# Q and K projected densely and read back into head slots, gated tiles paired in a bank, VectorE units in the first two chunks dropped

## The chip, the cores and the metric

The kernel runs on one core of a Trainium2 chip. The metric is the device time of one execution in microseconds. Four compute engines matter: TensorE (PE in the profile; PEld is its weight load), ScalarE (ACT), VectorE (DVE) and GpSimd (POOL). SyncE (SP) issues all the DMAs of this kernel.

## The reference

A transformer layer over S = 2048 rows of D = 640, H = 32 heads of Dh = 20, F = 1728, all in bf16:

```python
h  = x + attention(layernorm(x), wqkv) @ wo     # softmax(q k^T * 20**-0.5) v, not causal
z  = layernorm(h)
h2 = h + ((z @ w_gate) * (z @ w_up)) @ w_down
```

The layernorms have no weights. The scores are 32 x 2048 x 2048 values; their exponentials are the largest single piece of work.

## The kernel before, in words

**Slots.** A head has only 20 rows, so Q and K are kept transposed with each head in a slot of 32 partitions (`SLOT`), four heads to a group of 128 partitions, eight groups (`NG`). Row 20 of a slot holds a constant, 1 for K and `BETA` = 394 for Q, so that each score gets the same offset; rows 21 to 31 are zero. `qa[g]` holds the first three blocks of 512 queries, `qb[g]` the fourth, `kT[g]` all keys. V lies with the keys on the partitions in `vx`, 21 columns a head, the last of them a one, so that P·V also gives the softmax sums.

**Iterations.** The middle of the kernel is a sequence of iterations, one exponential on ScalarE each (L658). A unit is 128 keys by 512 queries of one head. Its scores are one matmul over the slot's 32 rows (L650); the units of different heads that are issued together use different row quarters of TensorE. Iterations take three units (128x1536, tile `sc0`) and two units (128x1024, `sc1`) in turn; the results are the `E` tiles, four and three of them. Some units don't go to ScalarE: `on_dve` (L366) says how many of a segment are computed by VectorE. Their score goes into a bank of a two-bank ring `mi`, from which L670 converts it to 16-bit integers (`di`); two such units make a batch of three more VectorE steps (L553 `dm`, L555 `dt`, L558 the product), and the exponential is the sum of the products of `dt` and `di` with V. `due` spreads these units over the iterations of their segment.

**Segments.** A segment is a head group with a range of keys and of queries. Query block 0 runs first: for groups 0 to 3 (`G1` = 4) key chunk by key chunk (four chunks of 512 keys), then groups 4 to 7 over all keys. Blocks 1 to 3 follow, each with some groups over 512 queries and the rest in two halves of 256.

**P·V and its end.** The products (L788) of one segment go into the only `acc` bank, 32 columns a head. `close` (L803) copies it into `asb` (L812), a single buffer for 512 queries. `norm` (L681) then runs on SP and POOL: the sums are written to DRAM (L688) and read back spread over partitions (L689), eight iterations later POOL takes the reciprocal (L692), it is written (L694) and read back broadcast with four DMAs (L697), and nine iterations after that POOL scales `asb` into `On` (L701), which frees `asb`.

**The queue of jobs.** Between the scores of iterations TensorE gets other work from one ordered queue (`add`, `do`, `peek`): transposes of the layernormed rows, projections, output projection (`job_out`), the gated layer (`job_glu`, L1098) and the down projection (`job_y`, L1111). A planner at build time keeps modelled clocks for TensorE and VectorE and issues a job's next piece when it fits; where the queue is empty it fills with matmuls on `ident` whose result isn't used. `ensure(key)` forces a job to its end when an iteration or a product needs its result. All matmuls of these jobs go through `by_cols` (L267), which splits 128 output rows into four pieces of 32, each on its own column quarter; a job uses one `mi` bank, evacuated by VectorE.

**Projections.** `job_proj` (L321) makes Q or K of one group and one chunk of 512 rows: five 128-row steps times four column pieces, 20 matmuls, from weights `wpad` in which each head's 20 columns are spread to slots of 32. `evac_b` adds the constant row (L245) and writes the slot layout. The padded weights are made from `wqk` by copies on ScalarE and POOL (`pad_half`) for all eight groups; `wqk` lies in tiles borrowed from `E` and `wo`. The padding tiles are zeroed by memsets on VectorE (L180). `job_V` (L333) makes one half of V for 128 rows. Order in the queue: per chunk the transposes, then V half 0 and Q, K of groups 0 to 3 in turn; then groups 4 to 7 of block 0 and of K, with V half 1; then Q of blocks 1 to 3, with the loads of `wo` (four DMAs a group, L962) behind the Q jobs of block 1; then one `spill` step per group, which copies Q to DRAM (`qsp`), where a slower fallback path can read it. Before block 3, `load_res` puts gated weights of four column groups into the tiles of `qa`.

**Gated layer and tail.** For two 128-row tiles at a time (256 columns), `glu_sum` (L1079) computes one 128-column block of `up` or `gate` in one bank: 27 weight blocks of 128 columns or 64, of which the up ones are copied to `u` (L238) and the gate ones multiplied with it (L1093). The last two tiles of block 3 are done after all exponentials; there (`last_tail`, from L1173) matmuls are 128 wide instead of 4 x 32.

## Time and profile before

| | |
|---|---|
| median of 3 executions | 891.98 us (890.58 to 893.82) |
| the profiled execution | 893.23 us |
| its span | 891.3 us |
| mean granted TensorE clock | 0.992 |
| instructions | 34572 |
| busy: PE, VectorE, ScalarE, POOL | 836.2, 717.6, 805.9, 196.2 us |
| DMA | 52.04 MB, mean 58 GB/s |

How to read the rows. In the groups a row is: line, engine, operation, output tile and input tile, shapes and types, count; then total busy time and the mean of one in ns; then the idle time of the engine right before these instructions and what ended most of it. In the timeline a row is: start, length (us), engine, line, operation, tiles, shape, and how many instructions were merged in the row; what it waited for stands in brackets. The table of windows has, for each stretch, its length, the busy time and count of PE, PEld, VectorE, ScalarE and POOL (or, where one line is asked for, of that line's engine alone), then the mean granted clock, the DMA share and GB/s. The digits of the slices are busy tenths in 40 equal parts of the span. The row for a DMA line gives issue times; the one of an engine's waits gives who waited for whom and for how long.

### The profile page before, as it was taken

To read this page: it belongs to the slowest core of one execution; us is meant where nothing else is said; L and a number is where in the kernel's file an instruction comes from. 1 tells how busy PE (TensorE), PEld (TensorE's weight loads), DVE (VectorE), ACT (ScalarE), POOL (GpSimd) and SP (SyncE) were. 2 spreads that over 40 slices of the span, in tenths; PEclk is the share of its full clock that TensorE was granted. 3 is DMA by queue.
4 is the path that set the end of the run, shared out by engine and by line. 5 is a ranking of instruction groups with operands and counts; after the bars stand their busy time and mean duration, and the time that the engine had idled before them with its cause. 6 is when DMAs were issued, how large, how long until landed. Compare 5 with 4: busy or idle time off the path is not lost.

```text
span 891.3 us, 34572 instructions
## 1 busy us (share of the span) xinstructions
PE 836.2 (94%) x15346; PEld 410.1 (46%) x15346; DVE 717.6 (81%) x1470; ACT 805.9 (90%) x719; POOL 196.2 (22%) x263
## 2 busy tenths in 40 slices
PE   6899999998989899999999999999999999999997
PEld 4334343332324334445445555555444555555775
DVE  7684578998879988987989889888987899888642
ACT  5899999998999999999999999999998999999431
POOL 3210034221123321221312233112310242113000
PEclk8999999998999999999999999999999999999999
DMA  6000001010053152101323132303600320031310
GB/s 200 9 25 1 3 16 40 20 36 12 14 203 104 42 146 74 37 17 31 95 70 95 29 92 71 96 22 98 154 4 22 88 55 16 10 104 39 82 46 19
DMA packets 85883, 52.04 MB, mean 58 GB/s; under 512 B 23664, under 2 KB 82592, under 8 KB 85728
## 3 DMA queue, kind: packets, MB, share of 16 engines
q1 hardware_dynamic: 85728, 49.77, 20.6%
q8 instruction: 122, 2.00, 1.0%
q14 instruction: 33, 0.27, 0.1%
HBM read 42.43 MB, written 7.31 MB: 56 GB/s over the span
## 4 chain that ended last, share of the span: by engine, by line
PE 54%; DVE 24%; ACT 18%; issue 3%; DMA 1%; SPq 0%; POOL 0%; ACTq 0%; DVEq 0%; POOLq 0%
PE mi L267 23%; ACT E L658 18%; PE sc L650 13%; PE acc L788 11%; DVE di L670 7%; DVE di L558 3%; PE f L267 3%; DVE dm L553 2%; DVE st L199 2%; DVE dt L555 2%; PE mi L650 1%; DVE hh L1093 1%; DVE qa L245 1%; DVE kT L245 1%; PE acc L1260 1%
## 5 line engine op out<-in xcount | busy, mean ns | idle before, releaser
L658 ACT ACTIVATE E<-sc 128x1536 bf16<-128x1536 f32 (+2 forms) x683 | 788.4, 1253 | 29.1 <-PE sc L650 13.4
L670 DVE TENSOR_SCALAR di<-mi 128x512 int16<-128x512 f32 x342 | 232.9, 684 | 47.5 <-PE mi L650 42.8
L788 PE MATMUL acc<-E,vx 128*32 128x256 bf16 (+1 forms) x2540 | 222.6, 315 | 5.7 <-DVE asb L812 2.3
L650 PE MATMUL sc<-qa,kT 32*128 32x256 bf16 (+1 forms) x1808 | 206.4, 320 | 11.3 <-ACT E L658 8.1
L650 PEld LDWEIGHTS <-kT 32*128 32x128 bf16 x3072 | 84.6, 91 | 219.9 <-issue 211.9
L692 POOL TENSOR_TENSOR rr<-rr,powers 128x8 f32<-128x8 f32 (+1 forms) x44 | 97.4, 2214 | 284.1 <-DMA rr<-sums 284.1
L788 PEld LDWEIGHTS <-vx 128*32 128x32 bf16 x3604 | 84.1, 95 | 104.3 <-issue 94.1
L558 DVE TENSOR_TENSOR di<-di,dm 128x1024 bf16<-128x1024 bf16 x171 | 120.4, 704 | 3.6
L650 PE MATMUL mi<-qa,kT 32*128 32x256 bf16 (+1 forms) x368 | 96.0, 312 | 4.3 <-DVE qa L245 2.2
L267 PE MATMUL mi<-lnT,wp 128*32 128x512 bf16 x1240 | 90.7, 385 | 2.3 <-DVE di L670 0.9
L553 DVE TENSOR_SCALAR dm<-di 128x1024 int16<-128x1024 int16 x171 | 77.5, 453 | 2.9
L788 PE MATMUL acc<-di,vx 128*32 128x256 bf16 (+1 forms) x532 | 77.4, 307 | 0.1
L788 PE MATMUL acc<-dt,vx 128*32 128x256 bf16 (+1 forms) x532 | 76.0, 309 | 0.3 <-DVE dt L555 0.3
L555 DVE TENSOR_SCALAR dt<-di 128x1024 int16<-128x1024 int16 x171 | 72.9, 426 | 0.0
L650 PE MATMUL sc<-qb,kT 32*128 32x256 bf16 (+1 forms) x732 | 66.8, 288 | 4.2 <-ACT E L658 3.5
L267 PE MATMUL mi<-wd,hh 128*32 128x320 bf16 x1391 | 65.6, 300 | 1.0 <-DVE xr L1123 0.9
L267 PE MATMUL mi<-ln2T,wu 128*32 128x256 bf16 (+1 forms) x1170 | 54.6, 298 | 5.3 <-DVE ln2T L238 2.2
L267 PE MATMUL mi<-ln2T,wg 128*32 128x256 bf16 (+1 forms) x1170 | 54.8, 298 | 0.5 <-DVE u L238 0.3
L267 PEld LDWEIGHTS <-hh 128*32 128x32 bf16 (+1 forms) x1489 | 46.1, 96 | 18.7 <-issue 9.5
L1093 DVE TENSOR_TENSOR hh<-mi,u 128x256 bf16<-128x256 f32 (+1 forms) x84 | 38.9, 463 | 11.3 <-PE mi L267 10.4
L267 PEld LDWEIGHTS <-wp 128*32 128x32 bf16 x1240 | 31.0, 96 | 35.2 <-issue 19.4
L238 DVE CAST u<-mi 128x256 bf16<-128x256 f32 (+1 forms) x84 | 38.9, 464 | 9.6 <-PE mi L267 8.2
(130 smaller groups left out, 759.9 us busy)
## 6 DMA issues: line engine op xcount, KB each, us to landing
wu<-in_B_w_up_dram SPq DMA_DIRECT2D x29, 320.0 KB
wg<-in_B_w_gate_dram SPq DMA_DIRECT2D x29, 320.0 KB
bc<-scr SPq DMA_DIRECT2D x64, 64.0 KB
bc<-scr SPq DMA_DIRECT2D x112, 32.0 KB
qsp<-qa SPq DMA_DIRECT2D x8, 384.0 KB
xr<-in_A_x_dram SPq DMA_DIRECT2D x16, 160.0 KB
out_dram<-xr SPq DMA_DIRECT2D x14, 160.0 KB
wd<-in_B_w_down_dram SPq DMA_DIRECT2D x13, 160.0 KB
```

The source lines that it names most:

```text
L199: nc.vector.bn_stats(st[:, h, :], halves[h] if halves else src[:, h * HALF:(h + 1) * HALF])
L238: nc.vector.tensor_copy(dst, src)
L267: nc.tensor.matmul(out[k:k + w, :], lhsT=lhsT[:, k:k + w], rhs=rhs, **flags)
L553: nc.vector.tensor_scalar(m16[:, 0:n], s16, M_MASK, M_BITS, ALU.bitwise_and, ALU.bitwise_or)
L555: nc.vector.tensor_scalar(t16[:, 0:n], s16, E_MASK, E_BITS, ALU.bitwise_and, ALU.bitwise_or)
L558: nc.vector.tensor_tensor(sb[:, 0:n], sb[:, 0:n], mb[:, 0:n], ALU.mult)
L650: nc.tensor.matmul(dst[:, h * w:(h + 1) * w], lhsT=kT[g][SLOT * j:SLOT * (j + 1), (kt + h) * P:(kt + h + 1) * P], rhs=q_of(g, b, c0, w)[SL ...
L658: nc.scalar.activation(e[:, 0:n], sc[:, 0:n], ACT.Exp, bias=EXP_BIAS, scale=SM_SCALE)
L670: nc.vector.tensor_scalar(t[:, k * BANK:(k + 1) * BANK], sd[:], EXP_A, 0.0, ALU.mult, ALU.max)
L692: nc.gpsimd.tensor_tensor(ri, r16, powers[:, 1:2].to_broadcast([P, n]), ALU.pow)
L788: nc.tensor.matmul(acc["t"][SLOT * j:SLOT * (j + 1), 0:w], lhsT=vx[kt][:, VS * h:VS * h + SLOT], rhs=e, start=(j not in acc["new"]), stop= ...
L1093: nc.vector.tensor_tensor(st["hh"][2 * fp + f2][0:M, c0:c0 + n], ps[0:M, 0:n], hold["u"][0:M, 0:n], ALU.mult)
```

## The change

It has three parts that share tiles.

**Dense projections.** Q and K of most groups are no longer computed slot by slot. `job_dense(m, t, ch)` computes 128 dense columns (6.4 heads) of Q (m = 0) or K (m = 1) for one chunk, 20 matmuls straight from `wqk`; five such tiles replace eight jobs. VectorE copies the bank to `dn` (four buffers), and a DMA writes it to a DRAM tensor `dense[m]`. Once all tiles of a set of groups are written, `read_slots` reads them back with four DMAs, one for each head of a group, 20 rows x groups x 512, into the slots. `kT`, `qa` and `qb` become one tile each over all groups. The constant rows are filled at the start: two memsets of 128x1024 on VectorE, and eight DMAs. Groups 0 to 3 of chunk 0, and K of group 0 in chunk 1, stay with `job_proj`, so only four groups of weights are padded (`GP`), in five copies instead of ten. Scores contract over 21 rows of a slot (`VS`) instead of 32, since rows 21 to 31 are no longer written. `ensure_qk` forces the dense tiles and the read-back of a set that is needed. The queue has K tiles, then V half 0 for each chunk; then the other dense tiles of block 0 and of K; then all of V half 1; then dense Q of blocks 1 to 3 with the last three `wo` loads in block 1; then five `wo` loads and one `spill` step of eight DMAs of 21-row slices.

**Gated layer.** With 256 columns, two weight blocks of the same kind share a bank side by side (`glu_bank`, `job_glu`): one copy of 128x512 for `up`, one product of 128x512 for `gate`. The last column group has 128 + 64 columns; its 64-column blocks of up and gate share one bank, above each other. `hh` gets one tile per column group.

**VectorE units.** `D_CHUNK` was 2 for each group in chunk 3 alone; it is now 0 in chunks 0 and 1 and 2 in chunks 2 and 3.

```diff
-CHUNK_D = (3, 0)
-D_CHUNK, D_WHOLE, D_HALF, D_LAST = 2, 12, 6, 4
+GP = 4
+D_CHUNK = (0, 0, 2, 2)
+D_WHOLE = (12, 12, 12, 12)
+D_HALF = (0, 6, 6, 6)
...
+    dense = [dram.tile([D, S], BF16, name=f"dense{m}", bufs=1) for m in range(2)]
-    wqk = [e_tile(c) for c in range(KT)]
-    wpad = [ra.tile([P, 2, H, SLOT], BF16, name=f"wp{c}") for c in range(KT)]
+    wqk = [ra.tile([P, D], BF16, name=f"wqk{c}") for c in range(KT)]
+    wpad = [ra.tile([P, 2, GP * HPG, SLOT], BF16, name=f"wp{c}") for c in range(KT)]
...
+    for m, v in ((1, 1.0), (0, BETA)):
+        src = dp.tile([P, DW], I16, name="di", bufs=3)[:].bitcast(BF16)
+        nc.vector.memset(src, v)
...
+                nc.sync.dma_start(dst[DH:P:SLOT, g0:g1, x:x + w], src[DH:P:SLOT, None, 0:w].to_broadcast([HPG, g1 - g0, w]))
...
+    def job_dense(m, t, ch):
+        yield ROUND * KT
+        ps = bank()
+        for c in range(KT):
+            for k in range(0, P, SLOT):
+                col = t * P + k
+                nc.tensor.matmul(ps[k:k + SLOT, :], lhsT=wqk_half(c, col // HALF)[:, m, col % HALF:col % HALF + SLOT],
+                                 rhs=lnT[:, c, ch * QB:(ch + 1) * QB], start=(c == 0), stop=(c == KT - 1))
+            mm(ROUND)
...
+        dn = dnp.tile([P, QB], BF16, name="dn")
+        nc.vector.tensor_copy(dn[:], ps[:])
+        nc.sync.dma_start(dense[m][t * P:(t + 1) * P, ch * QB:(ch + 1) * QB], dn[:])
+        written[m, t, ch] = clk["dve"] + WRITE
+        for it in slot_sets:
+            if it["m"] == m and it["ch"] == ch and all((m, x, ch) in written for x in it["ts"]) and not it["on"]:
+                later(3, lambda it=it: read_slots(it))
...
+    def read_slots(it):
...
+        src = dense[m][:, ch * QB:(ch + 1) * QB].rearrange("(g j e) n -> j e g n", j=HPG, e=DH)
+        for j in range(HPG):
+            nc.sync.dma_start(dst[SLOT * j:SLOT * j + DH, g0:g1, c0:c0 + QB], src[j, :, g0:g1, :])
+        for key in it["keys"]:
+            done.add(key)
+            ready[key] = max([clk["pe"]] + [written[m, t, ch] for t in it["ts"]]) + READ
+
+    def ensure_qk(key):
+        if key not in done and key in slot_of:
+            it = slot_of[key]
+            for t in it["ts"]:
+                ensure(("dn", it["m"], t, it["ch"]))
+            read_slots(it)
+        ensure(key)
+        clk["pe"] = max(clk["pe"], ready.get(key, 0))
...
-            return D_CHUNK * int((lo // TPB, g) >= CHUNK_D)
+            return D_CHUNK[lo // TPB]
...
-                    lhsT=kT[g][SLOT * j:SLOT * (j + 1), (kt + h) * P:(kt + h + 1) * P],
-                    rhs=q_of(g, b, c0, w)[SLOT * j:SLOT * (j + 1), :],
+                    lhsT=kT[g][SLOT * j:SLOT * j + VS, (kt + h) * P:(kt + h + 1) * P],
+                    rhs=q_of(g, b, c0, w)[SLOT * j:SLOT * j + VS, :],
...
+    for m in (1, 0):
+        slots(m, G1, NG, 0)
+    for ch in range(1, NB):
+        slots(1, int(ch == 1), G1, ch)
+        slots(1, G1, NG, ch)
+        slots(0, 0, NG, ch)
...
+            if ch == 1:
+                add(need_T(("k", 0, ch), ch), job_proj(1, 0, ch))
+            for t in range(3):
+                dense_job(1, t, ch)
+            for t in ts:
+                value(t, 0)
...
+    for t in range(2, KT):
+        dense_job(0, t, 0)
+    for ch in range(NB):
+        for t in range(2 + (ch > 0), KT):
+            dense_job(1, t, ch)
+    for t in range(NT):
+        value(t, 1)
...
+        for t in range(KT):
+            dense_job(0, t, b)
+            if b == 1 and t + KT < NG:
+                do(("wo", t + KT), lambda g=t + KT: load_wo(g))
...
+        for j in range(HPG):
+            rows = slice(SLOT * j, SLOT * j + VS)
+            nc.sync.dma_start(qsp[j, :, :, 0:QA], qa_all[rows, :, :])
+            nc.sync.dma_start(qsp[j, :, :, QA:S], qb_all[rows, :, :])
...
-    def glu_sum(st, fp, f2, k, c0, n, hold):
+    def glu_bank(st, parts, c0, n, use):
...
+        for k, (col, tiles) in enumerate(parts):
+            w = SLOT if end["pool"] is None else P // len(tiles)
+            for c in range(KT):
+                r0 = 0
+                for wt, f0, m in tiles:
+                    for x in range(0, m, min(w, m)):
+                        d = min(w, m)
+                        nc.tensor.matmul(ps[r0 + x:r0 + x + d, col:col + n], lhsT=wt[:, c, f0 + x:f0 + x + d],
+                                         rhs=st["ln2T"][:, c, c0:c0 + n], start=(c == 0), stop=(c == KT - 1))
+                    r0 += m
...
+            elif fp == FP - 1:
+                yield from glu_bank(st, [(0, [(wu, 0, P)]), (n, mixed)], c0, n, up(fp, 0, n))
+                yield from glu_bank(st, [(0, [(wg, 0, P)])], c0, n, gate(fp, 0, 1))
+            else:
+                for w, use in ((wu, up(fp, 0, None)), (wg, gate(fp, 0, 2))):
+                    yield from glu_bank(st, [(f2 * n, [(w, f2 * P, P)]) for f2 in range(2)], c0, n, use)
```

More of the change, by code (lines that the diff above doesn't have):

```diff
@@ L1082, in glu_sum @@
         yield ROUND * KT * n // QB
         ps = bank()
[L1084 to L1096 removed]
+        last = len(parts) * KT
@@ L1098, in job_glu, with up, use @@
+        use(ps)
     def job_glu(st, ts, order=tuple(range(FP))):
         c0, n = ts[0] * P, len(ts) * P
-        hold = {}
+        per = QB // n
+        u_of = {}
+        def up(fp, f2, odd):
+            def use(ps):
+                u = u_of[fp] = late["s"].tile([P, QB], BF16, name="u")
+                w = n * min(per, 2)
+                evac("dve" if end["pool"] is None else "act", u[:, 0:w], ps[:, 0:w])
+                ev(w, held["slot"])
+                if odd is not None:
+                    half(fp, u, odd, ps)
+            return use
```

165 lines of the change are left out of this document (91 added, 74 removed).

## The prediction

> **What bounds the kernel now.** I read the page first (span, slices, chain), then the groups by form, ScalarE's idle time by stretches, and the timeline of both ends.
>
> ```profile
> span 891.3 us, 34572 instructions
> ACT  5899999998999999999999999999998999999431
> PE 54%; DVE 24%; ACT 18%; issue 3%; DMA 1%; SPq 0%; POOL 0%; ACTq 0%; DVEq 0%; POOLq 0%
> L658 ACT ACTIVATE E<-sc 128x1536 bf16<-128x1536 f32 x341 | 500.4, 1467 | 11.7 <-PE sc L650 7.4 <-PE mi L650 2.7
> L658 ACT ACTIVATE E<-sc 128x1024 bf16<-128x1024 f32 x341 | 355.0, 1041 | 17.3 <-PE mi L650 8.2 <-PE sc L650 6.0
> L658 ACT ACTIVATE E<-sc 128x512 bf16<-128x512 f32 x1 | 0.6, 597 | 0.0
> 17.95 3.71 ACT L658 ACTIVATE E<-sc 128x1536 bf16<-128x1536 f32 x3 [1.45 <-PE sc L650]
> 833.41 0.60 ACT L658 ACTIVATE E<-sc 128x512 bf16<-128x512 f32 x1
> ```
>
> The exponentials run from 17.95 to 834.0 us and ScalarE idles before them for only 11.7 + 17.3 = 29.0 us. So there are three parts: a head of 18 us, a stage that ScalarE bounds (816 us; TensorE only sets the 29), and a tail of 891.3 - 834.0 = 57.3 us in which ScalarE hardly matters. That PE has 54% of the chain says only that the chain passes through it between two exponentials. One iteration (one exponential with its scores) is (1467 + 1041) / 2 = 1.254 us.
>
> **The change part by part.** The profiled execution took 893.23 us, 1.25 above the median of 891.98; the sum is a difference and is applied to both.
>
> *DVE units.* 8 more of the 128x512 units go to VectorE, so ScalarE runs 340 + 339 exponentials instead of 341 + 341 + 1: 1467 + 2 x 1041 + 597 = 4.15 us less. This stage is ScalarE's: **-4.2**.
>
> *Projections.* The matmuls of Q and K fall from 1240 to 140 + 720 = 860.
>
> ```profile
> 203.71 1.26 PE L267 MATMUL mi<-lnT,wp 128*32 128x512 bf16 x20
> L245 DVE TENSOR_SCALAR kT<-mi,kb 128x512 bf16<-128x512 f32 x31 | 23.0, 743 | 19.1 <-PE mi L267 19.1
> 834.73 10.27 PE L267 MATMUL mi<-ln2T,qa 128*32 128x256 bf16 x300
> L670 DVE TENSOR_SCALAR di<-mi 128x512 int16<-128x512 f32 x342 | 232.9, 684 | 47.5 <-PE mi L650 42.8
> ```
>
> A job of 20 takes 1.26 us, so 380 fewer are 24 us of TensorE. 62 evacuations of 0.743 become 7 of them and 36 plain copies (0.684, by the di row, the same shape out of the same bank): 46.1 to 29.8 us. Against that VectorE gets 8 x 0.684 us of new units and four more three-step batches. All of it lies beside exponentials and is worth nothing by itself; it lets the queue of jobs be empty earlier, which counts in the tail.
>
> *Gated layer.* Pairing leaves the matmul count as it was, but the two 64-column pieces now fill one bank: 5 rounds less for each pair of tiles (20 matmuls take 10.27 / 15 = 0.68 us, so up to 0.7 us each), and two evacuations of half a bank become one of a whole (0.68). Beside ScalarE this can only thin out the late scores. Ends: -6 (a third of the 17 us of ScalarE idle time after 225 us) and +3 (gated jobs now stand where the queue was empty). I take **-2**, near nothing, since most of these gaps end on a score matmul behind a VectorE unit, and those stay.
>
> *A disturbed stretch.*
>
> ```profile
> 200.00:225.00 25.00, 20.81 (x19) 0.86 0.04 12
> 225.00:250.00 25.00, 24.49 (x22) 1.00 0.16 53
> 204.50 1.64 DVE L558 TENSOR_TENSOR di<-di,dm 128x1024 bf16<-128x1024 bf16 x1
> 206.85 0.37 PE L650 MATMUL mi<-qa,kT 32*128 32x512 bf16 x1 [1.57 <-DVE qa L245]
> 210.00:212.00 2.00, 2.00 (x19) 0.42 (x23) 1.95 (x4) 1.36 (x2) 0.00 (x0) 0.50 0.00 0
> ```
>
> The first two rows are the exponentials alone: 24.49 - 20.81 = 3.7 us were lost where a slow VectorE step held the evacuation of a projection, TensorE idled 1.57 us, and its granted clock then was 0.50. After the change no projection runs past iteration 139 (this was about 150). It may recur with another evacuation: ends -3.7 and 0, taken **-2**.
>
> The Trainium skill ("TensorE: Matmul & The Clock Gate", HAM oscillation) puts the gap that drops the clock above about 3.4 us; here 1.57 us was enough, and the trace decides. By the page a late read-back of 2 us would cost 2 us, by this row 2 + 3.7.
>
> *The read-back.* K of groups 1 to 3 of chunk 1 has the least time: in the changed program its third dense tile ends just before scores 26 and the first use is scores 32, 6 x 1.254 = 7.5 us.
>
> ```profile
> 119.42 0.62 SPq L688 DMA_DIRECT2D sums<-part  x1
> 121.21 0.35 SPq L689 DMA_DIRECT2D rr<-sums  x1
> 825.66 1.73 SPq L697 DMA_DIRECT2D bc<-scr  x4
> 830.17 0.73 POOL L701 TENSOR_TENSOR part<-ash,bc 128x256 bf16<-128x256 f32 x1 [1.51 <-DMA bc<-scr]
> 0.00:25.00 25.00, 6.37 (x6) 0.86 0.59 178
> ```
>
> A write may be read 121.21 - 119.42 = 1.8 us after its issue; four reads take 1.73 us to issue and the last lands 830.17 - 827.39 = 2.8 us later. With the copy (0.7) and 128 KB instead of 8 at 178 GB/s (0.7) that makes 7.7 us against 7.5 plus the exponential in hand (1.25). Ends 0 and 5.7 (a 2 us gap with the clock's price); taken **+0.3**. All other sets are written 11 iterations or more ahead.
>
> *Late V.* The second half of V moves behind the dense K. The program forces five V jobs in one iteration (102), because a VectorE unit needs key tile 13.
>
> ```profile
> 26.11 0.86 PE L267 MATMUL mi<-wv,lnT 128*32 128x320 bf16 x20
> ```
>
> 5 x 0.8 = 4 us of TensorE against 2.5 us of exponentials in hand, with 0.8 us for the scores and products around it: **+2.5** (ends +0.5 and +4).
>
> *Spill and norm chain.* The spill now is 8 DMAs of 2.75 MB, queued on SP behind 20 loads of wo and the last read-back, and right ahead of a group's sums.
>
> ```profile
> L962 SPq DMA_DIRECT2D wo<-in_A_wo_dram x32: 281/328/1073, 175.3 to 196.1; - x32
> 243.75 0.50 SPq L688 DMA_DIRECT2D sums<-asb  x1
> 256.70 0.77 SPq L694 DMA_DIRECT2D scr<-rr  x1
> 264.54 1.27 POOL L701 TENSOR_TENSOR on<-asb,bc 128x512 bf16<-128x512 f32 x1 [12.86 <-DMA bc<-scr]
> 252.00:254.00 2.00, 1.98 (x34) 0.69 (x31) 1.97 (x6) 2.00 (x3) 0.00 (x0) 1.00 1.02 381
> DVE asb L812 <- POOL on L701: 2.7, 1, 2.7
> 268.00:270.00 2.00, 2.00 (x23) 0.41 (x16) 1.99 (x4) 1.72 (x2) 0.00 (x0) 1.00 0.18 28
> ```
>
> Before, the chain from sums to scaled output took 22.1 us, 11 of them the spill's; VectorE then waited 2.7 us in the next copy of the only asb buffer, and ScalarE lost 2.00 - 1.72 = 0.3. After: 20 x 0.33 + 1.7 + 2.8 + 2.75 MB / 381 GB/s = 7.2 make 18 us from the last dense tile, 11 more to the scaled output, and the next copy comes some 27 us after it: a wait of 2 to 3 us again. Ends 0 and +10 (rival A); **+1**.
>
> *Head.* Two 128x1024 fills precede the five wp fills, which halve.
>
> ```profile
> 0.94 0.38 DVE wp L180
> 2.57 0.38 DVE wp L180
> 3.16 0.80 DVE st L199 x2
> ```
>
> These are links of the chain: 384 elements each 0.41 us (start to start), statistics right behind. At that rate +2 x 1.09 - 5 x 0.2 = **+1.1** (0 if a fill costs half as much per element). The other fills and their DMAs end before their rows are used.
>
> *Tail.*
>
> ```profile
> 844.81 1.69 PE L267 MATMUL mi<-wd,hh 128*32 128x320 bf16 x44
> 846.43 0.31 PE L1183 MATMUL f<-xr,ident 128*128 128x320 bf16 x1
> 852.58 5.87 PE L267 MATMUL f<-wd,hh 128*128 128x320 bf16 x42
> 858.48 0.49 DVE L1123 TENSOR_TENSOR xr<-f,xr 128x320 bf16<-128x320 f32 x1 [1.41 <-PE f L267]
> 858.89 0.79 DVE L223 TENSOR_SCALAR ln<-xr,m,rstd 128x640 bf16<-128x640 bf16 x2
> ```
>
> Behind the last scores stand 20 + 300 gated matmuls now; in the changed program 60, all ahead of the last products. So L1183 starts not 846.43 - 834.0 = 12.4 us after the last exponential but after 0.8 (last products) and 80 down matmuls at 1.69 / 44 = 2.7 (overlapped ends taken off): 3.5, **-8.9**. The fill behind it shrinks from 3 + 42 full-width matmuls to 8 + 28 (0.14 us each): -1.3 us on the last L1123, behind which the layernorm at 858.89 stands: **-1.2**. The last gated layer saves one of 28 banks and ends on a wider evacuation: **-0.3**. Tail: -10.4; ends -11.5 and -8.
>
> Sum: -4.2 - 2 - 2 + 0.3 + 2.5 + 1 + 1.1 - 10.4 = -13.7 us: 879.5 beside 893.2, or **878** beside the median.
>
> **The rivals.**
>
> A. *The spill is slow.* If its 21-row DMAs move at the head's 178 instead of 381 GB/s, 2.75 MB take 15.5 us, and VectorE waits some 11 us in its copy. Two ring banks and the exponential in hand cover about 5; the other 6 stop ScalarE, and the idle clock adds 3.7. That is +9.7 in place of +1: **887**. For it: SP runs in order and asb is single; against it: 2.7 us cost almost nothing before.
>
> The Trainium skill ("DMA: Bandwidth & Descriptors", Why a DMA increments its semaphore by 16 and not by 1) lets a DMA use the largest number of engines up to 16 that divides both slowest dimensions: 7 for the spill's 21 and 168 rows, 10 for the 20-row reads. By it the spill would take an estimated 16.5 us, which is rival A; no row here shows a DMA of 21 rows.
>
> B. *Nothing gained.* The 260 gated matmuls (8.9 us) that leave the tail delay scores by as much in the stage, with V and the head on top and no recovered stretch: -4.2 + 8.9 + 2.5 + 1.1 - 10.4 + 1.3 = -0.8: **891**. Against it: the changed order fills 300 more dummy matmuls (kT,ident), so TensorE has the room.
>
> C. *Slower.* Scores on 21 of a slot's 32 rows no longer run side by side. Three now take 0.39 us; one after another they would add up to 2 x 0.21 us to each of 679 iterations. TensorE has some 7% free (836.2 of 891.3 is an upper bound of its work), 0.09 us an iteration; from there on the time grows, to **1000** or more. Against it: each slice still starts at its 32-row slot, and the tile form is unchanged. The rows:
>
> ```profile
> PE 836.2 (94%) x15346; PEld 410.1 (46%) x15346; DVE 717.6 (81%) x1470; ACT 805.9 (90%) x719; POOL 196.2 (22%) x263
> 44.03 0.39 PE L650 MATMUL sc<-qa,kT 32*128 32x512 bf16 x3
> ```
>
> **How the numbers follow.** Forecast (872 to 884) 0.55, A 0.22, B 0.15, C 0.08. The range for 8 in 10 runs from 870 (gated -6, stretch -3.7, V +0.5) to 891, past A and to the middle of B; it leaves out C, half of B and a little of the forecast's low side. Within 0.3% (2.7 us, about what a measurement can tell) is half of B, the rest of B splits evenly: faster 0.55 + 0.22 + 0.04 = 0.81, same 0.07, slower 0.04 + 0.08 = 0.12.
>
> **What would show it.** 679 exponentials of 340 and 339, idle 26 to 30 us before them; L1183's counterpart 3 to 4 us behind the last exponential; first exponential at 19; a gap of 2 to 3 us near 146 us (iteration 102); read-back waits under 1 us at scores 32. Wrong, if the copy of asb waits over 5 us, if score matmuls take more than 0.39 us for three, or if a stretch shows a clock of 0.5 beyond the head.

## The result, and the profile after

The changed kernel takes 924.6 us (median of 4, 920.2 to 937.8) against 891.4 us: a ratio of 1.035, interval 1.029 to 1.042. It is slower; 878 with a range of 870 to 891 was forecast. The profiled execution took 921.2 us. One of the four executions, of 937.8 us, was of a slower kind that now and then occurs whatever the kernel; such executions are left out of all medians below, so the changed kernel stands there with 921.2 us, and e11 and e17, whose profiles fell on them, have no losses in the table.

The page of the changed kernel, its span and ScalarE's slices:

```profile
span 919.3 us, 34241 instructions
ACT  4899987996399999999989999999999999999820
```

Its groups by form, and from its timeline the first and the last exponential and the first matmul of the last two tiles (L1305, which was L1183):

```profile
L725 ACT ACTIVATE E<-sc 128x1536 bf16<-128x1536 f32 x340 | 500.0, 1471 | 18.3 <-PE sc L717 10.2 <-PE mi L717 6.1
L725 ACT ACTIVATE E<-sc 128x1024 bf16<-128x1024 f32 x339 | 354.0, 1044 | 46.0 <-PE mi L717 36.2 <-PE sc L717 6.7
```

```profile
20.18 3.71 ACT L725 ACTIVATE E<-sc 128x1536 bf16<-128x1536 f32 x3 [1.62 <-PE sc L717]
868.62 1.45 ACT L725 ACTIVATE E<-sc 128x1536 bf16<-128x1536 f32 x1
874.30 0.31 PE L1305 MATMUL f<-xr,ident 128*128 128x320 bf16 x1
```

The slices have a hole (the 3) that the kernel before doesn't have. ScalarE's idle time before exponentials is 64.3 us (18.3 + 46.0), where 29.0 were shown before. To place it, the exponentials alone were taken by stretches: length of the stretch, then ScalarE's busy time in it. The kernel before:

```profile
17.95:130.00 112.05, 108.51 (x95) 1.00 0.03 9
130.00:156.00 26.00, 24.94 (x23) 1.00 0.18 41
156.00:219.00 63.00, 57.07 (x50) 0.95 0.10 24
219.00:254.00 35.00, 34.49 (x32) 1.00 0.24 82
254.00:834.01 580.01, 563.43 (x488) 1.00 0.26 67
```

The changed kernel:

```profile
20.18:130.00 109.82, 106.32 (x93) 1.00 0.20 59
130.00:156.00 26.00, 17.59 (x16) 0.87 0.23 57
156.00:219.00 63.00, 61.97 (x55) 1.00 0.41 105
219.00:254.00 35.00, 12.23 (x12) 0.66 0.19 54
254.00:870.07 616.07, 589.12 (x508) 0.99 0.24 63
```

Length less busy time is what ScalarE lost. Start, busy time (788.4 and 787.2), losses and tail add up to the span, so each part of the 28.0 us has its place:

| part | before | after | difference | forecast |
|---|---|---|---|---|
| start of the exponentials | 17.95 | 20.18 | +2.2 | +1.1 |
| exponentials | 788.4 | 787.2 | -1.2 | -4.2 |
| lost up to 130 us | 3.5 | 3.5 | 0 | 0 |
| lost 130 to 156 (read-back, V) | 1.1 | 8.4 | +7.4 | +2.8 |
| lost 156 to 219 (disturbed stretch) | 5.9 | 1.0 | -4.9 | -2 |
| lost 219 to 254 (spill) | 0.5 | 22.8 | +22.3 | +1 |
| lost behind 254 (gated layer among the scores) | 16.6 | 27.0 | +10.4 | -2 |
| tail | 57.3 | 49.2 | -8.1 | -10.4 |

**The hole.** From the timelines of VectorE, SP, GpSimd, TensorE and ScalarE, in order of time:

```profile
196.29 0.68 DVE L879 COPY asb<-acc 128x512 f32<-128x512 f32 x1
196.82 7.45 SPq L1040 DMA_DIRECT2D wo<-in_A_wo_dram  x20
205.89 0.93 SPq L1053 DMA_DIRECT2D qsp<-qa  x1
218.72 2.26 SPq L1054 DMA_DIRECT2D qsp<-qb  x1
221.07 1.44 SPq L755 DMA_DIRECT2D sums<-asb  x1
228.43 0.35 SPq L756 DMA_DIRECT2D rr<-sums  x1
238.97 1.26 POOL L768 TENSOR_TENSOR on<-asb,bc 128x512 bf16<-128x512 f32 x1 [5.01 <-DMA bc<-scr]
240.27 0.69 DVE L879 COPY asb<-acc 128x512 f32<-128x512 f32 x1 [21.76 <-POOL on L768]
241.01 0.61 PE L855 MATMUL acc<-dt,vx 128*32 128x512 bf16 x2 [21.36 <-DVE asb L879]
242.27 1.02 ACT L725 ACTIVATE E<-sc 128x1024 bf16<-128x1024 f32 x1 [20.81 <-PE mi L717]
```

`asb` is filled at 197.0, but its sums stand on SP behind 20 loads of `wo` and the spill, and are issued at 221.1. The next copy into the only `asb` is ready at 240.27 - 21.76 = 218.5 and waits for POOL's scaling; TensorE stops at the first product behind it, and with it the scores, which are queued in order. The table of windows (PE, PEld, VectorE, ScalarE, POOL, granted clock, DMA share, GB/s) shows the spill moving 151 GB/s at a share of 0.45, and, while TensorE stands, a clock of 0.50:

```profile
218.00:220.00 2.00, 1.65 (x22) 0.57 (x22) 0.51 (x1) 2.00 (x3) 0.00 (x0) 1.00 0.45 151
226.00:228.00 2.00, 0.00 (x0) 0.00 (x0) 0.00 (x0) 0.00 (x0) 0.00 (x0) 0.50 0.34 99
```

**130 to 156 us.** SP, TensorE and ScalarE:

```profile
125.15 0.34 SPq L363 DMA_DIRECT2D dense<-dn  x1
130.12 1.72 SPq L764 DMA_DIRECT2D bc<-scr  x4
131.89 1.50 SPq L386 DMA_DIRECT2D kT<-dense  x4
135.49 0.60 PE L717 MATMUL mi<-qa,kT 21*128 21x512 bf16 x1 [2.75 <-DMA kT<-dense]
137.23 1.45 ACT L725 ACTIVATE E<-sc 128x1536 bf16<-128x1536 f32 x1 [3.09 <-PE sc L717]
147.57 2.32 PE L281 MATMUL mi<-wv,lnT 128*32 128x320 bf16 x60 [0.29 <-DVE vx L252]
151.31 23.15 ACT L725 ACTIVATE E<-sc 128x1024 bf16<-128x1024 f32 x20 [3.52 <-PE mi L717]
```

The read-back that is late is that of K, chunk 3, groups 4 to 7, and who waits is a score into `mi`, so a unit for VectorE: these are the last 12 units of a segment, with key tiles 13 to 15, but they are issued from its first iterations on. The write of its last dense tile is issued at 125.15 us, the read at 131.89, behind the softmax chain of another group on SP, and the score that needs it starts at 135.49, 10 us behind the write. The same units force V up to tile 13, the second gap.

**Behind 254 us.** Who ended ScalarE's waits there (us in total, times, longest), before and after:

```profile
ACT E L658 <- PE mi L650: 7.1, 24, 0.9
ACT E L658 <- PE sc L650: 5.4, 16, 0.9
```

```profile
ACT E L725 <- PE mi L717: 16.7, 34, 1.7
ACT E L725 <- PE sc L717: 5.9, 19, 0.7
```

Nearly all of the +10.4 lies in waits that end with a score into `mi`, that is, of a unit for VectorE; gaps too short to count as waits make up the rest of the 16.6 and 27.0.

**Head.** The memsets put everything behind them 1.1 us later. Another 0.9 us comes from two subtractions that now run beside GpSimd's padding copies; after, then before:

```profile
1.01 0.91 DVE L179 MEMSET di<- 128x1024 bf16 x1 [1.01 <-PEq L1502]
7.70 0.72 POOL L207 COPY wp<-wqk 128x640 bf16<-128x640 bf16 x1 [3.56 <-DMA wqk<-in_A_wqkv_dram]
7.75 0.85 DVE L243 TENSOR_SCALAR xs<-xs,m 128x640 bf16<-128x640 bf16 x1
8.69 0.91 POOL L207 COPY wp<-wqk 128x640 bf16<-128x640 bf16 x1 [0.28 <-DMA wqk<-in_A_wqkv_dram]
8.93 0.84 DVE L243 TENSOR_SCALAR xs<-xs,m 128x640 bf16<-128x640 bf16 x1
```

```profile
6.64 0.37 DVE L229 TENSOR_SCALAR xs<-xs,m 128x640 bf16<-128x640 bf16 x1
```

The start of the exponentials varies between executions: in the six profiles with the old head (before, e5, e7, e9, e14, e15) it lies at 16.8 to 17.95 us, in five with the new one (changed, e1 to e4) at 19.4 to 20.2.

### The profile page after: what moved, and what is told of

Read it like the earlier page. It is cut to its first block, busy times and chain, and to the rows that moved or that the text cites. A ratio compares the mean times of both kernels' runs of the same rounds, so it can differ in the third digit from the quotient of the medians.

```text
span 919.3 us, 34241 instructions
## 1 busy us (share of the span) xinstructions
PE 831.0 (90%) x15185; PEld 405.9 (44%) x15185; DVE 710.8 (77%) x1402; ACT 803.4 (87%) x708; POOL 197.7 (22%) x258
## 3 DMA queue, kind: packets, MB, share of 16 engines
q1 hardware_dynamic: 96336, 58.44, 23.9%
## 5 line engine op out<-in xcount | busy, mean ns | idle before, releaser
L725 ACT ACTIVATE E<-sc 128x1536 bf16<-128x1536 f32 (+1 forms) x679 | 787.2, 1258 | 64.3 <-PE mi L717 42.2
L717 PE MATMUL sc<-qa,kT 21*128 21x256 bf16 (+1 forms) x1800 | 206.7, 322 | 16.7 <-ACT E L725 13.7
L717 PEld LDWEIGHTS <-kT 21*128 21x128 bf16 x3072 | 85.4, 92 | 225.4 <-issue 214.3
L717 PE MATMUL mi<-qa,kT 21*128 21x256 bf16 (+1 forms) x376 | 99.6, 315 | 4.6 <-DMA kT<-dense 2.8
L717 PE MATMUL sc<-qb,kT 21*128 21x256 bf16 (+1 forms) x732 | 67.1, 291 | 4.7 <-ACT E L725 4.6
L281 PE MATMUL mi<-wd,hh 128*32 128x320 bf16 (+1 forms) x1432 | 67.2, 300 | 1.8 <-DVE hh L1207 0.7
L281 PE MATMUL mi<-kT,ident 128*32 128x512 bf16 x608 | 43.7, 395 | 1.2 <-DVE di L737 0.9
L1175 PEld LDWEIGHTS <-wu 128*32 128x32 bf16 (+1 forms) x1230 | 35.1, 99 | 20.7 <-issue 14.9
L1175 PEld LDWEIGHTS <-wg 128*32 128x32 bf16 (+1 forms) x1230 | 33.9, 96 | 13.6 <-issue 8.8
L1207 DVE TENSOR_TENSOR hh<-mi,u 128x512 bf16<-128x512 f32 (+1 forms) x48 | 31.7, 660 | 9.9 <-PE mi L1175 9.3
```

What stands on the lines that cost most here:

```text
L281: nc.tensor.matmul(out[k:k + w, :], lhsT=lhsT[:, k:k + w], rhs=rhs, **flags)
L717: nc.tensor.matmul(dst[:, h * w:(h + 1) * w], lhsT=kT[g][SLOT * j:SLOT * j + VS, (kt + h) * P:(kt + h + 1) * P], rhs=q_of(g, b, c0, w)[SLO ...
L725: nc.scalar.activation(e[:, 0:n], sc[:, 0:n], ACT.Exp, bias=EXP_BIAS, scale=SM_SCALE)
L1175: nc.tensor.matmul(ps[r0 + x:r0 + x + d, col:col + n], lhsT=wt[:, c, f0 + x:f0 + x + d], rhs=st["ln2T"][:, c, c0:c0 + n], start=(c == 0), ...
L1207: nc.vector.tensor_tensor(st["hh"][fp][:, f2:f2 + k, c0:c0 + n], g, u, ALU.mult)
```

## The experiments

Theory after the first look: three causes, namely the queue in front of the sums, the order of K and V, and a third behind 254 us, at first taken to be pairing. All times are medians. "Lost" is ScalarE's loss by the same stretches; it and the tail are read from one profiled execution, whose time can lie some us off the median (e7's took 896.5 us, its median is 899.4).

| kernel | time | lost 130-156 | lost 219-254 | lost behind 254 | tail |
|---|---|---|---|---|---|
| before | 891.4 to 893.2 | 1.1 | 0.5 | 16.6 | 57.3 |
| changed | 921.2 | 8.4 | 22.8 | 27.0 | 49.2 |
| e1 no spill | 906.6 | 9.0 | 6.8 | 25.5 | 51.7 |
| e2 spill spread | 910.9 | 8.7 | 7.5 | 34.3 | 49.3 |
| e3 K, V order | 905.7 | 0.8 | 13.2 | 28.1 | 49.5 |
| e4 unpaired | 933.4 | 8.6 | 23.6 | 30.9 | 55.4 |
| e5 before, 21 rows | 892.6 | 1.9 | 0.3 | 15.5 | 58.6 |
| e6 32 rows | 918.7 | 8.3 | 22.8 | 25.4 | 49.2 |
| e7 before, paired | 899.4 | 1.9 | 0.2 | 27.2 | 49.5 |
| e8 mended | 884.8 | 0.7 | 0 | 23.6 | 47.6 |
| e9 before, units | 908.3 | 1.0 | 0.6 | 23.9 | 70.0 |
| e10 mended, unpaired | 893.7 | 0.7 | 0 | 26.8 | 52.9 |
| e11 order, 21 rows | 890.5 | - | - | - | - |
| e12 mended, wait | 894.9 | 0.7 | 0 | 30.5 | 52.1 |
| e13 mended, old units | 895.9 | 1.0 | 0.2 | 25.0 | 52.3 |
| e14 before, paired + units | 902.4 | 1.2 | 0.6 | 37.1 | 50.7 |
| e15 before, shifted | 903.9 | 1.2 | 0.1 | 27.0 | 60.8 |
| e16 mended, late fills | 883.5 | 0.9 | 0 | 23.2 | 48.0 |
| e17 e16, EARLY 7 | 895.0 | - | - | - | - |
| e18 e16, EARLY 5 | 898.7 | 0.9 | 0 | 34.6 | 50.9 |

**e1, the spill left out.**

```diff
-        for j in range(HPG):
-            rows = slice(SLOT * j, SLOT * j + VS)
-            nc.sync.dma_start(qsp[j, :, :, 0:QA], qa_all[rows, :, :])
-            nc.sync.dma_start(qsp[j, :, :, QA:S], qb_all[rows, :, :])
```

> The changed kernel with the eight spill DMAs left out (Q isn't copied to DRAM, so the fallback path would have nothing to read; the fast path's output needs no spill). Theory: the 2.75 MB in front of the sums of group 4 make the whole stop of TensorE and ScalarE at 219 to 242 us (ScalarE lost 22.8 us between 219 and 254 us). Then that stretch loses 1 us or less, the copy of asb waits 3 us at most, and the time falls by 21 to 24 us, to 898 to 902. Rival: the 20 loads of wo and the read-back that also stand in front of the sums on SP (196.8 to 205.9 us) are the larger part; then the copy of asb still waits over 8 us and the time stays above 908.

906.6 us: 15 less than 921.2, not 21 to 24, and between the two expectations. VectorE's waits from 200 to 270 us, and SP's row of the sums:

```profile
DVE asb L879 <- POOL on L768: 5.5, 1, 5.5
```

```profile
206.46 0.52 SPq L755 DMA_DIRECT2D sums<-asb  x1
```

The sums now go at 206.5 instead of 221.1, and the copy of `asb` still waits 5.5 us. Both readings hold in part: 16 of the 22.3 us are the spill's, and 6 remain without it. Ahead of the sums there still stand the `wo` loads and the read-back; no run takes only these away.

**e2, the spill spread.** Each of the eight DMAs by `later`, four iterations apart.

```diff
+            later(4 * (2 * j + 1), lambda rows=rows, j=j: part_a(rows, j))
+            later(4 * (2 * j + 2), lambda rows=rows, j=j: part_b(rows, j))
```

> The changed kernel with the same eight spill DMAs, of the same bytes and forms, issued four iterations (5 us) apart instead of in one step. Theory: only their standing together ahead of one group's sums costs time; each alone (504 or 168 KB, 3.3 or 1.1 us at 155 GB/s) delays a chain by no more than that, and the time is that of the kernel without the spill, within 2 us. Rival: a slow spill costs wherever it lies, since each of the chains of the next 40 us is late; then it is 4 to 10 us above the kernel without the spill, and copies of asb wait several us more than once.

The stretch up to 254 us loses 7.5 us, as without the spill (6.8), so standing together was the harm. The median, 910.9, is 4.3 us above e1's, but single executions overlap (907.7 to 917.0 against 903.9 to 909.3), and what the profile loses more it loses behind 254 us, where the spill is over.

**e3, K of chunk 3 and V of tiles 13 to 15 first.**

```diff
-    for ch in range(NB):
+    for ch in (NB - 1, *range(NB - 1)):
...
-    for t in range(NT):
+    for t in (13, 14, 15, *range(13)):
         value(t, 1)
```

> The changed kernel with two orders in the job queue turned: dense K of chunk 3 ahead of that of chunks 0 to 2, and V half 1 of key tiles 13 to 15 ahead of tiles 0 to 12. Theory: both gaps of 130 to 156 us (ScalarE lost 8.4 us there) have one root, VectorE's units of group 4, which are the last 12 of a segment but are issued at its start and need the last key tiles; then ScalarE loses 1 to 2 us there and the time falls by 6 to 8 us, to 914 to 919, the spill's stop being untouched. Rival: the work of this stretch is too much for TensorE whatever its order; then the loss only moves to another iteration and the time falls by less than 2 us.

The loss from 130 to 156 us fell from 8.4 to 0.8, as the theory has it. The time fell by 15, though, since the spill's stop shrank with it:

```profile
DVE asb L879 <- POOL on L768: 14.4, 1, 14.4
```

In this order the sums of one group are issued ahead of the `wo` loads, and only the next group's meet the spill. That the stop would stay was wrong: its size is set by which group's sums arrive at SP in front of what.

**e4, unpaired.**

```diff
-        per = QB // n
+        per = 1
```

> The changed kernel with the gated layer of 256 columns back to one block a bank (128x256 copies and products, 27 banks for two tiles); the rest as it is. Theory: pairing makes VectorE's pieces and the ring's holds longer, and this is the 10 us that ScalarE loses more after 254 us than before the change (27.0 against 16.6); then that loss falls to 16 to 20 and the time by 7 to 11 us, to 914 to 918. Rival: the loss comes from the shifted order of the units and jobs, not from pairing; then ScalarE still loses 24 us or more after 254 us and the time stays within 3 us.

The loss behind 254 us didn't fall (30.9) and the tail rose by 6.2 us: 933.4, which neither side had. Pairing isn't the third cause by itself in this kernel.

**e5 and e6, rows.** The next idea was the clock: in e1 to e4 the granted clock is 0.5 in several stretches behind 400 us, in the kernel before in none. e5 edits the kernel before, e6 the changed one.

```diff
-                    lhsT=kT[g][SLOT * j:SLOT * (j + 1), (kt + h) * P:(kt + h + 1) * P],
-                    rhs=q_of(g, b, c0, w)[SLOT * j:SLOT * (j + 1), :],
+                    lhsT=kT[g][SLOT * j:SLOT * j + VS, (kt + h) * P:(kt + h + 1) * P],
+                    rhs=q_of(g, b, c0, w)[SLOT * j:SLOT * j + VS, :],
```

> The kernel before with one edit: its score matmuls take 21 rows of a slot instead of 32 (rows 21 to 31 are zeros, so the output is the same). The four kernels of the changed family run so far each show three to five stretches of granted clock 0.5 after 400 us, 3 to 12 us long, and ScalarE loses 25 to 34 us behind 254 us; the kernel before shows none there and loses 16.6. Theory: what sets the clock looks at how much of the array works, so scores of 21 of 32 rows lower it and the same short idle times of TensorE now make the clock drop; then such stretches appear here, ScalarE loses 6 to 15 us more, and the time is 898 to 908. Rival: the rows don't matter (three scores take 0.39 us with 21 rows as with 32) and the stretches come from the changed order of the jobs; then no clock of 0.5 appears behind 250 us and the time is that of the kernel before within 2 us.

```diff
-    for m, v in ((1, 1.0), (0, BETA)):
-        src = dp.tile([P, DW], I16, name="di", bufs=3)[:].bitcast(BF16)
-        nc.vector.memset(src, v)
...
+    def pattern(x, g0, g1, c0, v):
+        for g in range(g0, g1):
+            nc.gpsimd.tensor_copy(x[:, g, c0:c0 + QB], v[:, 0:1].to_broadcast([P, QB]))
+    for k, f in enumerate(fills):
+        later(3 + 2 * k, lambda f=f: pattern(*f))
```

> The changed kernel with scores over all 32 rows of a slot again. Rows 20 to 31 are written by GpSimd (the constant row and zeros, 512 columns a copy, one pair of groups every second iteration from the third on), in place of the two memsets on VectorE and the eight DMAs at the head. Theory that the rows set the clock: the stretches of clock 0.5 behind 400 us go, ScalarE loses 15 to 20 us behind 254 us instead of 27, and with 1 us less in the head the time falls by 8 to 12 us, to 912 to 917, the spill's stop being untouched. Rival, the order of the jobs: the stretches stay, and the time falls by 1 to 2 us only.

e5 is the kernel before (892.6, ratio 1.002, interval 0.999 to 1.006) and e6 loses 25.4 us behind 254 us, with the clock at 0.5 around 478 us as in the changed kernel. The rows matter neither for the matmuls nor for the clock; the theory fell, and with it the prediction's rival C. e6 gains 2.6 us: its exponentials start at 17.0 instead of 20.2 us, and 2 us of that are lost again before 130 us (5.6 instead of 3.5).

**e7, pairing alone in the kernel before** (`glu_bank`, `job_glu` and the `hh` tiles taken over).

```diff
-    def glu_sum(st, fp, f2, k, c0, n, hold):
+    def glu_bank(st, parts, c0, n, use):
```

> The kernel before with the paired gated layer alone. By the run without pairing, whose tail was 55.4 us long against 49.2 with it, pairing is worth 6 us of tail, and nothing was lost by it beside the exponentials; so 885 to 889. Rival: the tail is shorter in the changed kernel because its queue of jobs is empty earlier, and pairing alone only delays scores behind longer VectorE pieces: 890 to 897.

899.4, the rival's side and above its range. The exponentials alone behind 254 us:

```profile
254.00:845.13 591.13, 563.95 (x487) 0.99 0.26 67
```

27.2 us are lost instead of 16.6, and the tail is 49.5 instead of 57.3. By the order of its instructions 100 gated matmuls are left behind the last scores, where the kernel before has 320: 220 fewer stand in the tail and so as many more ahead of it, and the stage loses more (10.6) than the tail saves (7.8). That the one causes the other is the rival's reading; e10 and e15 below speak against it.

**e8, three causes mended together.** e6's and e3's edits, and:

```diff
+    def loads():
+        for g in range(KT):
+            later(5 * g + 1, lambda g=g: load_wo(g))
+    do(("wo",), loads)
...
+        def one(g):
+            nc.sync.dma_start(qsp[g][:, 0:QA], qa_all[:, g, :])
+            nc.sync.dma_start(qsp[g][:, QA:S], qb_all[:, g, :])
+        for g in range(NG):
+            later(3 * (g + 1), lambda g=g: one(g))
```

> The changed kernel with four edits: scores over 32 rows as in the run before last; dense K of chunk 3 and V of key tiles 13 to 15 first; the five late loads of wo five iterations apart instead of in one step; the spill by whole slots of 128 rows, one group (two DMAs) every third iteration. If the three causes are right (queue behind spill and wo loads 22.3, order 7.4, rows 10), their sum leaves the tail's gain of 8 and the units' gain: 919.3 - 22 - 7 - 10 = 880 of span, so 878 to 884, below the kernel before. If the rows aren't the third cause, 888 to 893.

884.8, between the two expectations; ratio 0.994 (0.991 to 0.997), so a little faster than the kernel before. Nothing is lost from 219 to 254 us; 23.6 still are behind it. At one place there, TensorE waits in order for VectorE's copy of `ln2T`, its clock drops to 0.5 and the scores are late; TensorE and ScalarE of e8:

```profile
531.56 1.47 PE L1181 MATMUL mi<-ln2T,wu 128*32 128x256 bf16 x24 [1.43 <-DVE ln2T L243]
534.48 2.46 ACT L716 ACTIVATE E<-sc 128x1536 bf16<-128x1536 f32 x2 [3.02 <-PE mi L708]
```

**e9, the units alone in the kernel before.**

```diff
-D_CHUNK, D_WHOLE, D_HALF, D_LAST = 2, 12, 6, 4
+D_CHUNK, D_WHOLE, D_HALF, D_LAST = (0, 0, 2, 2), 12, 6, 4
...
-            return D_CHUNK * int((lo // TPB, g) >= CHUNK_D)
+            return D_CHUNK[lo // TPB]
```

> The kernel before with the VectorE units of the chunks alone changed (none in chunks 0 and 1, two for each group in chunks 2 and 3, 8 more in all). By the term of the prediction, 4.2 us less of exponentials: 886 to 890. Rival: the eight units cost as much as they save, because each iteration with such a unit puts a fourth score and a bank of the ring in its way, and because the later iterations shift against the jobs; then 891 to 895, with ScalarE losing 3 us or more beyond the kernel before's 27.6.

908.3, outside both expectations: eight units moved cost 16 us. ScalarE's work fell as forecast, to 679 exponentials, but 540 gated matmuls now stand behind the last scores and the tail is 70.0 us. So what acts is less the work of the units than where the plan puts everything else.

**e10 and e11, the mended kernel taken apart.** e10 is e8 with `per = 1`; e11 is the changed kernel with e3's order, `wo` four and the 21-row spill six iterations apart.

> The mended kernel (32 rows, order, wo and spill spread) with the gated layer back to one block a bank. The kernel before with pairing alone took 899.4 us: its tail fell from 57.3 to 49.5 us, and ScalarE lost 27 us instead of 16.6 behind 254 us, since the 220 gated matmuls that left the tail now stand between scores. Theory: the same trade here, so without pairing ScalarE loses 16 to 19 us behind 254 us instead of 23.5, the tail is 54 to 57 us instead of 47.6, and the time is within 3 us of the mended kernel's 884.8. Rival: in the changed kernel the loss behind 254 us has another cause (the run without pairing still lost 30.8 us there); then it stays at 23 or more, the tail gets longer, and the time is 890 to 895.

> The changed kernel with its 21-row scores, memsets and fills as they are, and only the order mended: K of chunk 3 and V of tiles 13 to 15 first, the late wo loads four iterations apart, the eight spill DMAs of 21 rows six iterations apart. If rows don't matter (the two runs on rows), this is the mended kernel but for the head: ScalarE loses 3.5 us before 130 us (6.6 there, where GpSimd's fills were in the way) and starts 1.5 to 2 us later; 883 to 888. Rival: the slow DMAs of 21 rows still hold back a chain of sums wherever they lie; then copies of asb wait 4 us or more in sum and the time is 889 to 894.

e10 takes 893.7, the rival's side: unpaired, 26.8 us are lost behind 254 us and the tail is 52.9. It leaves 220 gated matmuls behind the last scores where e8 leaves 60, and yet loses more between them. Pairing is worth 9 us here and cost 7 in the kernel before. e11's 890.5 lies in its rival's range (889 to 894). The rival's mechanism isn't seen, though: in the profile that there is, no copy of `asb` waits for POOL's scaling from 150 to 850 us, and 0.6 us are lost from 219 to 254. Where the 6 us against e8 go stays open.

**e12, GpSimd's fills from iteration 16, and a gated job that waits for `ln2T`.**

```diff
+        until = clk["dve"] + 300
+        while len(ts) == 2 and end["pool"] is None and clk["pe"] < until and not forced["on"]:
+            yield WAIT
```

> The mended kernel with two more edits. GpSimd's fills start at iteration 16 instead of 3, behind the first layernorm: ScalarE loses 3.5 to 4.5 us before 130 us instead of 6.6. And a gated job doesn't start before VectorE's modelled time of the ln2T copy has passed, so that TensorE isn't held in order by that copy (1.43 us at 530 us in the mended kernel, then clock 0.5 and 3.0 us lost on ScalarE). Theory that this wait is what drops the clock late: no wait of TensorE on ln2T over 0.5 us, ScalarE loses 17 to 20 us behind 254 us instead of 23.5, time 878 to 881. Rival: the clock drops at other short idle times as well; then the loss stays at 22 or more and the time is 881 to 884.

The wait of 1.4 us is gone, and the loss behind 254 us rose to 30.5 us: 894.9, outside both expectations. That this wait is the late cause is not borne out; the edit also moves the gated jobs, so it doesn't test the wait alone.

**e13 to e16, burden or placement.** e13 is e8 with `D_CHUNK = (0, 0, 0, 2)`, e14 the kernel before with e7's and e9's edits, e16 e8 with the late fills but without the wait. e15 is the kernel before with

```diff
-LEAD, EARLY = 14, 6
+LEAD, EARLY = 14, 7
```

> The mended kernel with the VectorE units of the chunks as before the change (two per group in chunk 3 only). Moving these eight units alone cost the kernel before 16 us (908.3: ScalarE lost 7 us more behind 254 us and the tail was 70 us instead of 57.3). Theory U, the units as such are a burden of 7 us or more behind 254 us: without them ScalarE loses 14 to 18 us there instead of 23.5 and the time is 876 to 881, in spite of 4 us more of exponentials. Theory P, the stretch behind 254 us depends on how units, jobs and iterations happen to fall against each other, and the kernel before sits at a good place: the loss stays between 18 and 28 us, the time is 884 to 893.

> The kernel before with both parts that cost something alone: pairing (+7 us) and the eight units (+16 us). Theory U (each is a burden of its own): 910 to 916. Theory P (each only takes the plan away from its good place, and what pairing saves of the tail stays): the two don't add, 897 to 904, with 100 gated matmuls behind the last scores as with pairing alone (540 with the units alone, 320 before).

> The kernel before with one number changed, EARLY from 6 to 7: VectorE's units are due one unit earlier, and no work is added, removed or resized. By the plan, 440 gated matmuls instead of 320 stand behind the last scores. Theory P: this alone costs some of what the parts of the change cost; ScalarE loses 20 us or more behind 254 us instead of 16.6, or the tail is 59 us or longer, and the time is 895 to 903. Theory U: a shift without work is worth nothing, 890 to 894.

> The mended kernel with GpSimd's fills from iteration 16 on, without the wait before gated jobs. In the run with both edits ScalarE lost 4.5 us before 130 us instead of 6.6, but 30.5 behind 254 us instead of 23.5, and the tail was 52.1 instead of 47.6. If the wait did the harm (it moves gated jobs later), this run has the mended kernel's late loss and tail and 2 us less in front: 881 to 885. If the harm came with the shift in front: 888 to 895.

e13 takes 895.9, above both ranges: without the eight units nothing is won back, rather 11 us lost. e14 takes 902.4, as theory P has it: +7 and +16 alone, +10 together. e15 takes 903.9, 0.9 above P's range, with no work changed at all. The exponentials alone behind 254 us, e13 and then e15:

```profile
254.00:841.09 587.09, 562.09 (x485) 1.00 0.25 65
254.00:840.91 586.91, 559.95 (x486) 0.99 0.25 64
```

In e15 27.0 us are lost where it was 16.6, as many as in the changed kernel. All three speak for placement and against a burden of the units. e13 also shows that the clock isn't the late cause by itself: it loses 25.0 us there, and in stretches of 20 us its granted clock is 1.00 in every one. e16 takes 883.5, ratio 0.990 (0.987 to 0.993), the lowest median of all: the harm in e12 came with the wait, and 2 us less are lost up to 130 us.

**e17 and e18, the same shift of e16.**

> The best kernel so far (mended, fills from iteration 16, 883.5 us) with EARLY 7 instead of 6, the shift without work that cost the kernel before 11.5 us. By the plan 100 gated matmuls and 32 of the down projection stand behind the last scores instead of 60 and 80. If a placement that happens to fit is all that the mended kernel has over the kernel before, this run loses it, 890 to 900. If it is better than the kernel before at a like shift, it stays well below that kernel's 903.9 and near its own: 882 to 890.

> The same with EARLY 5; 140 gated matmuls and none of the down projection stand behind the last scores. Same two expectations: 890 to 900 if the placement is all, 882 to 890 if not; ScalarE loses 20 to 28 us behind 254 us in either case.

895.0 and 898.7, both in the range that was expected if the placement is all; e18 loses 34.6 us behind 254 us, more than either expectation had. A shift without work costs e16 11.5 and 15 us, as it cost the kernel before 11.5. So with EARLY 6 both kernels stand at the best of the placements tried. At equal settings, though, e16 is the lower one both times that can be compared: 883.5 against 892.4 with 6, 895.0 against 903.9 with 7. That the mended change is worth some 9 us at a like placement rests on these two pairs; the kernel before wasn't run with 5.

## Why the prediction was wrong

*Spill and norm chain: the step that failed most.* The mechanism is the text's own and rival A's; the size is not. +1 was taken, A priced 9.7, measured were 22.3 (16 with the spill, 6 without it, by e1). Three terms were off. The transfer was put at 381 GB/s and ran at 151 to 170 (212 to 224 us; A's 178 was near): the issues fill SP from 205.9 to 221.1. The sums then took 7.4 us from their issue to their read (1.7 in the kernel before), while the spill's own bytes were still moving; from the last dense tile, written at 196.7, to the scaled output it took 43 us, not 18 + 11. And the cover of 5 us that A allowed wasn't there: TensorE stood at the first product behind the copy, and of 21.8 us of waiting ScalarE lost 20.8. The DMA share of 0.45 agrees with the rule of the Trainium skill that the prediction weighed ("DMA: Bandwidth & Descriptors", Why a DMA increments its semaphore by 16 and not by 1): seven of 16 engines are 0.44. Two of the prediction's three signs of being wrong came true: the copy of `asb` waited 21.8 us, and the clock was at 0.5 beyond the head.

*Read-back and late V.* The set that was named has no wait in the trace. "All other sets are written 11 iterations or more ahead" is the false sentence: K of chunk 3 for groups 4 to 7 is read by VectorE's first units of group 4. It went by the order of the keys, not by which units go first. V's 2.5 us came out as 3.5. The first gap costs more than its 2.75 us, as the text had priced: the clock is at 0.5 from 134.8 to 141.7 us. e3 shows that both gaps come from the order.

*Gated layer: -2, and +10.4 measured.* The false step is that the gaps that end on a score behind a VectorE unit "stay": they grew from 7.1 to 16.7 us. Rival B had a mechanism for a loss here, matmuls that leave the tail and delay scores instead, and e7 looks like it, with 7.8 us of tail for 10.6 in the stage. It isn't shown to be the cause. e15 leaves 440 gated matmuls behind the last scores, more than the 320 of the kernel before, and loses 27.0 us all the same, and e10 loses more than e8 with more of them left. B's objection to itself held as a count (608 dummy matmuls on `kT,ident` instead of 312) and yet was no measure of room. e15 shows that this stage of the kernel before moves by 10 us when its units shift by one, so neither a -2 nor a +10 could be read from its terms.

*Units: -4.2.* Exponentials fell to 340 and 339 as said. The term added up their lengths, but these overlap: they sum to 856.0 us in the kernel before, and ScalarE was busy with them for 788.4. In busy time the term is about 3.8 (and an iteration 1.15 us, not 1.254). Their mean length then rose by 3 to 4 ns, 2.4 us over 679, and -1.2 was left. As a change by itself the step is worth +16 (e9), through the plan.

*Right.* The tail: L1305 starts 874.3 - 870.1 = 4.2 us behind the last exponential (3.5 forecast, 12.4 before), and the layernorm comes 885.55 - 874.30 = 11.3 us later instead of 12.5, the -1.2 of the text; the rest of the difference is the landing of the last output (6.7 us behind the last VectorE step instead of 5.1). The disturbed stretch is gone, for -4.9 instead of -2. Scores on 21 rows cost nothing (e5). Memsets: 1.1 as said, and another 0.9 from the collisions that came with them.

What stays open: what it is in a placement that makes the stage lose 16 or 27 us (the clock isn't needed for it, by e13), and which of the short waits of TensorE halve the clock. A placement that is good for the changed kernel's 21-row form wasn't looked for.

## What to carry to other kernels

Before moving bulk transfers on an in-order queue, write down which small latency chain stands behind them and whether its buffer is single: the price was 22 us with 2.75 MB and 20 loads in front. Spread over some iterations, the same bytes cost next to nothing (e2 beside e1), and with the loads spread too, in another order and form, nothing was lost (e8). A read-back or a forced job is due at its first user in issue order, and units sent to a second engine may be the first users of the last data. Where a build-time plan interleaves engines that are all over 75% busy (here TensorE, VectorE and ScalarE), shift it once without changing any work (here 11 to 15 us) before a term of 2 or 4 us in a sum is believed.

## What the runs showed of the hardware

A transfer over 21 partitions ran at a DMA share of 0.44 to 0.47 and 151 to 170 GB/s (212 to 224 us), where the spill over 128 partitions of the kernel before had 1.02 and 381.

The granted clock fell to 0.5 about waits of TensorE of 2.75 us (at 134.8 us) and, in e8, of 1.43 us (at 531.6 us), and stayed there for 6.8 and 3.4 us. The Trainium skill ("TensorE: Matmul & The Clock Gate", HAM oscillation) names gaps above about 3.4 us; in these rows shorter ones were enough. In e8 TensorE was partly idle already: it was busy for 0.63 of the stretch from 529 to 530 us and for 0.13 of the next. The prediction's wait of 1.57 us didn't stand alone either: from 205.3 to 208.0 us TensorE was busy for 0.6 us in all, and the clock fell at 207.5, in a second wait.

A bf16 128x640 subtraction on VectorE took 0.85 us instead of 0.37 beside a copy of GpSimd. The Trainium skill ("SBUF — State Buffer", Who interferes with whom) says that the two share a port pair that one holds for its whole instruction; the rows agree in so far as both subtractions end just behind the copy beside them (8.60 behind 8.42 us, 9.77 behind 9.60).
